# Scores on quarters of the array, a hand-computed order up to chunk 2, and left-over tokens kept on chip

## The chip, the cores and the metric

The kernel runs on one core of one Trainium2 chip. The metric is the device time of one execution in microseconds (us), the median over the runs of one kernel. A profiled execution of the same kernel has a time of its own. Within it the span runs from the first to the last instruction.

## The reference: what is computed

Three layers follow one another, all in float32: windowed attention and two gated feed-forward layers.

```python
# attention: q, k, v are (4, 8, 576, 64) = batch, head, token, head width
scores = q @ k.T / 8
# heads 0-3: keys 0..31 back; heads 4-7: keys 0..127 back, every fourth one
attn = softmax(where(mask, scores, -1e9)); a = attn @ v
x = a.transpose(0, 2, 1, 3).reshape(2304, 512)
# layer 1: w1, w2 (512, 1024), w3 (1024, 1024), w_out (1024, 512)
x = ((x @ w1) * (x @ w2)) @ w3 @ w_out
# layer 2: w_gate, w_val (512, 1536), w_out (1536, 512)
return (silu(x @ w_gate) * (x @ w_val)) @ w_out
```

The weights arrive as float64. Each matrix is kept as a high part and a rest, and a product is three matmuls: high by high, high by rest, rest by high (`mm3`, lines 225 to 227).

## The kernel before, in words

**Stages.** The product W = w3 @ w_out of layer 1 is computed first, in sixteen steps of twelve matmuls over 512 columns (`w_step`). Layer 1 then runs over five chunks of tokens, four of 512 and one of 256 (`stage1`). For each of eight slices k of the inner width a chunk has a gate `w1` (twelve matmuls), a gate `w2` (twelve) and a contraction with W (twelve). So a step of W, a gate or a contraction is twelve matmuls of 512 columns; the text calls it a unit. The W product is 16 units and each of the chunks 0 to 3 is 24. Layer 2 (lines 703 on) works with seven products in place of eight on quarters of the matrices. Its operands are made during layer 1 and kept in DRAM (`quarters`, eighteen blocks of weights, of which chunks 0 to 4 take 3, 4, 4, 5 and 2).

**Attention.** Sixteen pairs of heads, four to a batch. A pair's 576 queries are nine blocks of 64, each against 96 keys. `scores` computes one block of both heads in one matmul: the queries of the two heads stand side by side in a zero-padded 128-row tile, so the 128x128 array holds 64 rows of head 0 and 64 of head 1, with zeros in the other halves. A float32 matmul is two instructions in the trace. The scores are done in two groups, of five blocks and of four; then come mask and scale (DVE, line 344), maximum (347), exponential (ACT, 349), sum and reciprocal (352, 353), normalising (354; DVE for the first batch, POOL later), transposes on PE in three groups (367) with an ACT copy each, the product with v (382, in two groups, each matmul on half of the array's columns), and the split into high part and rest as the layer's input x (167, 168).

**Batches and chunks.** A batch has 576 tokens and a chunk 512, so each batch leaves 64 to 256 tokens for the next chunk. They go to DRAM (`x1d`, line 411) and are read back in front of the next chunk (`load_block`, kind x1).

**Conversion.** A block of weights is 1 MB, two float64 matrices of 128x512. One block takes an ACT pass (208) and two DVE passes (209, 210) to make float32, then an ACT pass (203) and a DVE pass (204) to split it. Twenty blocks are converted before and in chunk 0: eight of w3 and w_out pieces, four of further w3 pieces, eight of (w1, w2).

**Order.** The functions are called in program order; the compiler layer then orders each engine's instructions by its own timeline. All steps of W and the whole first batch of attention are called before the first gate:

```python
for s, step in enumerate(W_STEPS):
    while n_split[0] < min(W_NEEDS[s] + 1, N_W1) and free:
        next_block()
    w_step(*step)
    attend(min(4 * s + 5, done_at[1]))
attend(done_at[1])
```

In chunks 0 to 2 `between` calls pieces of the next batch's attention between the gates and contractions, and `rest` calls weight conversion behind them. SP issues nearly all DMAs from one queue; the stores of layer 1's result are issued by ACT. `stage1(3)` and `stage1(4)` and layer 2 follow.

Of the kernel before, what the change touches and what calls it, by code (L numbers as in the profile page):

```python
# [19 lines left out]
NT = B * S  # L20
# [3 lines left out]
P = 128  # L24
# [6 lines left out]
NBLK = S // QB  # L31
KT = DM // P
# [11 lines left out]
N_EARLY = 15  # L44

ATT_BY = 0.75


W_ORDER = [(("wo1", j), ("w3a", j)) for j in range(2)]
for _name, _j in ("w3c", 0), ("wo1", 2), ("w3a", 2), ("wo1", 4), ("w3a", 4), ("w3c", 2), ("wo1", 6), ("w3a", 6), ("w3d", 0), ("w3d", 2):  # L50
    W_ORDER.append(((_name, _j), (_name, _j + 1)))

W_STEPS = [("w3a", 0), ("w3a", 1), ("w3c", 0), ("w3c", 1), ("w3a", 2), ("w3a", 3), ("w3a", 4), ("w3a", 5),
           ("w3c", 2), ("w3c", 3), ("w3a", 6), ("w3a", 7)] + [("w3d", _j) for _j in range(4)]
W_NEEDS = [1, 2, 3, 4, 5, 5, 7, 7, 8, 9, 10, 10, 11, 11, 12, 12]
W_ORDER += [(("w1", k), ("w2", k)) for k in range(K1)]
# [23 lines left out]
NPROD = 7  # L80
A11, S1, S2, A12, S3, S4, A22 = range(NPROD)
# [8 lines left out]
QUARTERS = [3, 4, 4, 5, 2]  # L90


def moe_chain_kernel(tc, q_in, k_in, v_in, w_in, mask_in, out):
# [8 lines left out]
    with static as st, other as ot, psum as pp, dram as dp:  # L102
# [7 lines left out]
        wslot = [w_all[:, i] for i in (2, 3, 7, 4, 0, 6, 1, 5)] + [fp.tile([P, 2, 2, 512], F32R, name=f"W{i}") for i in range(4)]  # L110
# [3 lines left out]
        ost = [ot.tile([P, S], F32, name=f"o{i}") for i in range(2)]  # L114
        bank = [pp.tile([P, 512], F32, name=f"bk{i}") for i in range(8)]
        acc, ba, bb, batt = bank[:4], bank[4], bank[5], bank[6:]
        x1d = dp.tile([KT, P, NT], F32, name="x1d")
# [8 lines left out]
        for c, n in enumerate(QUARTERS):  # L126

            blocks += [("x1", c + 1)] if c < 4 else []
            blocks += [("w", i + j) for j in range(n)]
            i += n  # L130
# [3 lines left out]
        slot_of, pair_of, uses, raw_at = {}, {}, {}, {}  # L134
        free, raw_free = deque(), deque()

        x1_there = set()

        def load_block():
            n = n_loaded[0]  # L140
            if n == len(blocks) or not raw_free or (blocks[n][0] == "x1" and blocks[n][1] not in x1_there):
                return
# [4 lines left out]
            if kind == "w":  # L147
                dst = r.rearrange("p (b f) -> p b f", b=2)
                src = w_in[i]
            else:  # L150
                if kind == "x1":
                    a, size, ms = CHUNKS[i][0], REST * i, slice(0, KT)
                else:
                    a, size, ms = i[0] * TOK, TOK, slice(2 * i[1], 2 * i[1] + 2)
                dst = r[:, :(ms.stop - ms.start) * size].rearrange("p (m t) -> p m t", t=size)
                src = (x1d if kind == "x1" else x2d)[ms, :, a:a + size].rearrange("m p t -> p m t")
            for b in (0, 1) if n == 0 else (slice(None),):
                nc.sync.dma_start(out=dst[:, b], in_=src[:, b].bitcast(U32))

        def done_with(n):  # L160

            if any(raw_at[n] is r for r in raw[:2]) or n_loaded[0] < (N_W1 if raw_at[n] is raw[2] else N_EARLY):
                raw_free.append(raw_at[n])
# [11 lines left out]
        def next_block():  # L175
            n = n_split[0]
            n_split[0] += 1
            kind, i = blocks[n]
            if kind == "w":
                convert_weights(n, W_ORDER[i])  # L180
            else:
                size = REST * i
                r = raw_at[n].rearrange("p b f w -> p (b f w)")[:, :KT * size].bitcast(F32)
                r = r.rearrange("p (m t) -> p m t", m=KT)
                for m in range(0, KT, 2):
                    x = x_of(i)[:, :, m:m + 2, :size]
                    to_parts(r[:, m:m + 2], x[:, 0], x[:, 1])
            done_with(n)
# [741 lines left out]
```

## Time and profile before

| | us |
|---|---|
| median of 3 runs (lowest, highest) | 848.9 (845.47, 849.26) |
| the profiled execution's own time | 847.58 |
| its span | 845.6 |
| PE busy (x4954) | 825.4 (98% of the span) |
| weight loads busy (x4954) | 751.7 (89%) |
| DVE busy (x957) | 539.6 (64%) |
| ACT busy (x1009) | 429.4 (51%) |
| POOL busy (x124) | 89.2 (11%) |
| DMA | 207.09 MB, mean 245 GB/s |

PE is TensorE, DVE VectorE, ACT ScalarE, POOL GpSimd and SP the engine that issues DMAs. Matmuls are pipelined and their ends are modelled: a matmul of 512 columns is listed with about 0.39 us while the next one starts about 0.23 us later, so what one costs is read from start to start. Idle times of an engine stand with the instruction that ended the wait.

### The profile page before, as it was taken

What the parts mean: (1) busy time and instruction counts of PE and PEld (TensorE: products, weight loads), DVE (VectorE), ACT (ScalarE), POOL (GpSimd) and SP (SyncE); (2) the same over time, 40 slices, a digit from 0 to 9 for tenths busy, and PEclk for the clock granted to TensorE, in tenths of its full rate; (3) what the DMA queues carried; (4) which work ended last, traced back from release to release, by engine and by line L of the source; (5) the groups of instructions that cost most, each with busy time, mean ns of one, the idle gap of its engine ahead of it and who ended that gap; (6) DMA issues with size and microseconds to landing.
All of it is one profiled execution on the core that took longest, in us unless ns stands there. A gap on an engine that the chain in (4) does not pass through costs nothing.

```text
span 845.6 us, 13394 instructions
## 1 busy us (share of the span) xinstructions
PE 825.4 (98%) x4954; PEld 751.7 (89%) x4954; DVE 539.6 (64%) x957; ACT 429.4 (51%) x1009; POOL 89.2 (11%) x124
## 2 busy tenths in 40 slices
PE   7899899999999999999999999999999999999998
PEld 5777788888788788888899999999999999999997
DVE  5899856365626652476766646588655668464867
ACT  5688765455644645254555544354453454353532
POOL 1000134225510642000000000000000000000000
PEclk9999899999999999999999999999999999999999
DMA  9998638558756665567999877788978687887735
GB/s 271 340 354 252 217 88 263 178 171 273 223 164 203 208 209 165 192 223 245 324 299 370 299 253 248 249 289 281 327 249 270 230 266 248 297 283 249 248 102 174
DMA packets 93248, 207.09 MB, mean 245 GB/s; under 512 B 7424, under 2 KB 56704, under 8 KB 88448
## 3 DMA queue, kind: packets, MB, share of 16 engines
q1 hardware_dynamic: 90304, 201.53, 72.5%
q10 hardware_dynamic: 2880, 4.72, 1.6%
q8 instruction: 39, 0.64, 0.3%
q14 instruction: 25, 0.20, 0.1%
HBM read 162.45 MB, written 43.78 MB: 244 GB/s over the span
## 4 chain that ended last, share of the span: by engine, by line
PE 75%; DMA 9%; DVE 9%; ACT 4%; issue 2%; SPq 0%; ACTq 0%; DVEq 0%
PE bk L225 23%; PE bk L226 23%; PE bk L227 23%; DMA raw<-w_in 6%; PE bk L330 2%; ACT s L349 2%; DVE raw L210 2%; PE bk L382 2%; DVE w L204 1%; PE bk L367 1%; DVE raw L209 1%; DVE u L530 1%; DMA q<-q_in 1%; DMA raw<-x1d 1%; DVE early L210 1%
## 5 line engine op out<-in xcount | busy, mean ns | idle before, releaser
L225 PE MATMUL bk<-x,w 128*128 128x512 f32 (+2 forms) x400 | 146.6, 368 | 4.4 <-ACT ta L244 2.2
L226 PE MATMUL bk<-x,w 128*128 128x512 f32 (+2 forms) x400 | 146.7, 367 | 0.0
L227 PE MATMUL bk<-x,w 128*128 128x512 f32 (+2 forms) x400 | 146.4, 366 | 0.0
L225 PE MATMUL bk<-w 128*128 128x384 f32 (+1 forms) x264 | 92.3, 355 | 2.6 <-ACT w L203 2.6
L226 PE MATMUL bk<-w 128*128 128x384 f32 (+1 forms) x264 | 93.5, 354 | 0.8 <-DVE w L204 0.8
L227 PE MATMUL bk<-w 128*128 128x384 f32 (+1 forms) x264 | 90.3, 351 | 0.0
L225 PEld LDWEIGHTS bk<-x,w 128*128 128x128 f32 x400 | 75.5, 189 | 14.6 <-ACT ta L244 2.9
L797 DVE TENSOR_TENSOR acc<-bk,acc 128x384 f32<-128x384 f32 x102 | 55.8, 553 | 44.7 <-PE bk L227 44.5
L226 PEld LDWEIGHTS bk<-x,w 128*128 128x128 f32 x400 | 75.7, 189 | 9.7 <-DVE x L168 0.2
L227 PEld LDWEIGHTS bk<-x,w 128*128 128x128 f32 x400 | 75.7, 189 | 9.6
L227 PE MATMUL bk<-po,wo 128*128 128x384 f32 x240 | 80.6, 336 | 0.0
L226 PE MATMUL bk<-po,wo 128*128 128x384 f32 x240 | 80.3, 335 | 0.0
L225 PE MATMUL bk<-po,wo 128*128 128x384 f32 x240 | 79.5, 336 | 0.3 <-DVE acc L797 0.3
L530 POOL TENSOR_TENSOR stage<-raw,stage 128x256 fp32r<-128x256 f32 x88 | 62.5, 738 | 55.2 <-ACT stage L529 55.0
L722 ACT ACTIVATE u<-bk 128x384 f32<-128x384 f32 x80 | 38.6, 489 | 53.6 <-PE bk L227 53.6
L167 ACT ACTIVATE po<-u 128x768 fp32r<-128x768 f32 (+1 forms) x64 | 50.9, 803 | 26.2 <-PE bk L227 10.5
L208 ACT ACTIVATE raw<-raw 128x1024 f32<-128x1024 f32 (+1 forms) x33 | 37.3, 1130 | 51.6 <-DMA raw<-w_in 51.5
L168 DVE TENSOR_TENSOR po<-u,po 128x768 fp32r<-128x768 f32 (+1 forms) x64 | 57.4, 901 | 8.7 <-ACT po L167 8.6
L226 PE MATMUL bk<-p,W 128*128 128x512 f32 (+1 forms) x160 | 59.2, 374 | 0.0
L227 PE MATMUL bk<-p,W 128*128 128x512 f32 (+1 forms) x160 | 58.7, 371 | 0.0
L225 PE MATMUL bk<-p,W 128*128 128x512 f32 (+1 forms) x160 | 57.8, 375 | 0.1
L349 ACT ACTIVATE s<-s,sm 128x96 f32<-128x96 f32 x144 | 52.0, 364 | 11.4 <-DVE sm L347 11.0
(122 smaller groups left out, 1711.5 us busy)
## 6 DMA issues: line engine op xcount, KB each, us to landing
w<-wd SPq DMA_DIRECT2D x70, 512.0 KB, 4.4
wo<-wod SPq DMA_DIRECT2D x63, 512.0 KB, 4.6
raw<-w_in SPq DMA_DIRECT2D x31, 1024.0 KB, 9.5
mid<-wd SPq DMA_DIRECT2D x42, 512.0 KB, 4.6
wd<-stage SPq DMA_DIRECT2D x16, 896.0 KB, 6.5
wd<-u SPq DMA_DIRECT2D x8, 896.0 KB, 5.6
x<-wd SPq DMA_DIRECT2D x14, 512.0 KB, 4.7
v<-v_in SPq DMA_DIRECT2D x16, 432.0 KB, 8.1
```

What stands on the lines that cost most here:

```text
L167: nc.scalar.activation(hi, src, AF.Copy)
L168: return nc.vector.tensor_tensor(out=lo, in0=src, in1=hi.bitcast(F32), op=ALU.subtract)
L208: nc.scalar.activation(hi.bitcast(F32), hi.bitcast(F32), AF.Prelu, scale=REBIAS, alpha=SIGN_UP)
L210: nc.vector.scalar_tensor_tensor(out=lo, in0=hi, scalar=3, in1=lo, op0=ALU.logical_shift_left, op1=ALU.bitwise_or)
L225: nc.tensor.matmul(ps, wh, xh, start=start, stop=False, skip_group_check=onto)
L226: nc.tensor.matmul(ps, wh, xl, start=False, stop=False, skip_group_check=onto)
L227: nc.tensor.matmul(ps, wl, xh, start=False, stop=stop, skip_group_check=onto)
L330: nc.tensor.matmul(ps[:, (n - b0) * KW:(n - b0 + 1) * KW], q[:, QB + 2 * QB * n:QB + 2 * QB * (n + 1)], kk[:, n * QB:n * QB + KW], start=T ...
L349: nc.scalar.activation(s[:, n], s[:, n], AF.Exp, bias=m[:, 0, n:n + 1], accum_out=m[:, 1, n:n + 1])
L530: (nc.gpsimd if len(stages) == 2 else nc.vector).tensor_tensor(out=dst[:, :, 1], in0=src, in1=dst[:, :, 0].bitcast(F32), op=ALU.subtract)
L722: nc.scalar.activation(t, src, AF.Copy)
L797: nc.vector.tensor_tensor(out=a, in0=ps, in1=a, op=ALU.add)
```

## The change

Four things change, all before chunk 3.

1. **Scores on quarters.** The zero padding of the queries goes, with the memsets on POOL and one of two loads per pair. Each block of each head is a matmul of its own, 64 rows by 64 columns of the array: the head chooses the row half and the PSUM bank, the block's parity the column half. There are 18 such matmuls per pair in place of nine, issued in one go over two banks. The values are likewise issued in one go instead of two. Mask, maximum and so on now run per column group (four and five columns).
2. **An order computed in the kernel.** Everything up to the end of chunk 2 is built as nodes with an engine, an estimated time, what it comes after, and a due time. A list scheduler simulates the five engines and the DMA with those times and starts, on each free engine, the ready node with the earliest due time. The resulting order is issued as it is, without the compiler layer's reordering. Chunks 3 and 4 and layer 2 are still ordered by that layer.
3. **Another sequence.** The blocks of weights are ordered so that (w1, w2) 0 and 1 come third and fourth. Gates of chunk 0 are due from 36 us on and alternate with steps of W: two steps of W, then the gates k = 0 and 1, then again steps of W and gates k = 2, 3, and the rest of W, with results of four gates kept. Attention takes four PSUM banks until the first gate, then two. Quarter blocks in chunks 0 to 4 are 2, 5, 5, 4, 2.
4. **Left-over tokens on chip.** They stay in an SBUF tile `beyond` and are split from there; the DRAM tensor `x1d`, its stores and loads go. Stores of layer 1's result in chunks 0 to 2 are issued by SP in place of ACT.

```diff
-            def scores(i, g):
-                b0, b1 = (0, 5) if g == 0 else (5, 9)
-                for n in range(b0, b1):
-                    nc.tensor.matmul(
-                        ps[:, (n - b0) * KW:(n - b0 + 1) * KW],
-                        q[:, QB + 2 * QB * n:QB + 2 * QB * (n + 1)],
-                        kk[:, n * QB:n * QB + KW],
+            def scores(i, got):
+                q, kk = qd[i % 2], ks[i % 2]
+                for j, n in [(j, 2 * c + (z + j) % 2) for c in range(NHALF) for z in range(2) for j in (1, 0)] + [(1, NBLK - 1), (0, NBLK - 1)]:
+                    h = slice(j * D, (j + 1) * D)
+                    c, z = column(j, n)
+                    c = NHALF if n == NBLK - 1 else c % NHALF
+                    nc.tensor.matmul(
+                        banks_of[got[j]][z * QB:(z + 1) * QB, c * KW:(c + 1) * KW],
+                        q[h, n * QB:(n + 1) * QB], kk[h, n * QB:n * QB + KW],
                         start=True, stop=True,
                     )
...
+W_BLOCKS = [("wo1", 0, 10), ("w3a", 0, 4), ("w1", 0, 0), ("w1", 1, 1), ("wo1", 2, 11), ("w3a", 2, 5), ("w1", 2, 2),
+            ("wo1", 4, 6), ("w3a", 4, 8), ("w1", 3, 3), ("wo1", 6, 7), ("w3a", 6, 9),
+            ("w3b", 0, 4), ("w3b", 2, 5), ("w3b", 4, 4), ("w3b", 6, 5)] + [("w1", _k, _k) for _k in range(4, K1)]
-QUARTERS = [3, 4, 4, 5, 2]
+QUARTERS = [2, 5, 5, 4, 2]
+DMA_RATE = 0.31
+FIRST, EACH, START = 4, 6, 36.0
...
+            def run_nodes(stock):
+                wanted = [x["key"] for x in nodes]
+                for i in reversed(range(len(nodes))):
+                    for a in nodes[i]["after"]:
+                        wanted[a] = min(wanted[a], wanted[i] - nodes[a]["us"] - (4.0 if nodes[a]["mb"] else 0.2))
...
+                    for e in ready:
+                        if free[e] > t + 1e-9:
+                            continue
+                        for i in sorted(ready[e], key=lambda i: (wanted[i], i)):
...
+                            started.append(i)
+                            free[e] = t + x["us"]
...
+                with tc.manual_schedule(engines=set(ENGINES)):
+                    for i in started:
+                        x = nodes[i]
+                        x["f"](*x["args"], **({"got": x["got"]} if x["take"] else {}))
...
+            q_loads(0, 0)
+            mask_at = [node("SP", 0.47, load_mask, slice(0, NHALF), mb=0.2, key=0.1)]
+            for n in range(2):
+                conversion(n, 0.2 + 0.1 * n)
+            q_loads(1, 1)
+            v_loads(0, 2)
+            attention(0, FIRST, 6, mask_at)
...
+            gates(0, 0)
+            gates(0, 1)
+            for j in (2, 4):
+                w_steps(0, (j,), next_at())
+                w_steps(0, (j + 1,), next_at())
+                gates(0, 2 + (j - 2) // 2)
+            w_steps(0, (6, 7), next_at(2))
...
+            for i in range(NPAIR):
+                q_loads(NPAIR + i)
+                v_loads(NPAIR + i)
+                attention(NPAIR + i, START + T * (12 + 5 * i), 3 * T, started_gates)
...
+            def beyond_parts(c, key):
+                size = REST * c
+                ends = []
+                for m in range(0, KT, 2):
+                    before = x_at[c - 1][:] + x_use.get(c - 2, []) + ([raw_use[2], raw_use[3]] if c == 1 else [])
+                    h = node("ACT", on_act(2 * size), x1_part, c, m, 0, after=before, key=key)
+                    ends.append(node("DVE", on_dve(2 * size), x1_part, c, m, 1, after=[h], key=key))
...
-                if g == 1:
-                    nc.sync.dma_start(out=x1d[hp, :, b * S + own:(b + 1) * S], in_=o)
```

## Rows read from the trace of the kernel before

**Rows 1.** Busy time by stretch: stretch, its length, engines, PEclk, DMA share, GB/s.
```profile
0.00:40.00 40.00, 32.76 (x176) 24.22 (x177) 28.41 (x50) 23.25 (x56) 3.22 (x12) 0.91 1.00 300
40.00:100.00 60.00, 54.36 (x356) 44.16 (x355) 58.48 (x90) 50.35 (x101) 0.00 (x0) 0.94 0.82 270
100.00:347.00 247.00, 245.02 (x1594) 202.41 (x1593) 127.17 (x256) 131.99 (x419) 85.97 (x112) 1.00 0.62 198
347.00:450.00 103.00, 101.28 (x581) 89.91 (x580) 70.77 (x147) 50.72 (x111) 0.00 (x0) 1.00 0.80 265
450.00:846.00 396.00, 392.00 (x2254) 391.04 (x2252) 254.79 (x416) 173.12 (x323) 0.00 (x0) 1.00 0.77 259
```

**Rows 2.** Timeline of PE, 0 to 92 us: start, us, instruction [idle before it <- what ended that].
```profile
9.73 3.43 PE L330 MATMUL bk<-k,q 128*128 128x96 f32 x18 [2.32 <-DMA q<-q_in]
...
27.40 0.68 PE L225 MATMUL bk<-w 128*128 128x512 f32 x1 [1.54 <-ACT w L203]
...
89.75 1.22 PE L225 MATMUL bk<-x,w 128*128 128x512 f32 x2 [2.13 <-ACT x L167]
```

**Rows 3.** The same around the end of chunk 2.
```profile
349.50 0.39 PE L227 MATMUL bk<-p,W 128*128 128x512 f32 x1
349.73 0.39 PE L225 MATMUL bk<-x,w 128*128 128x512 f32 x1
...
354.49 0.39 PE L225 MATMUL bk<-x,w 128*128 128x512 f32 x1
```

**Rows 4.** The same around one group each of scores, transposes and values.
```profile
120.61 2.14 PE L330 MATMUL bk<-k,q 128*128 128x96 f32 x18
122.54 0.48 PE L225 MATMUL bk<-x,w 128*128 128x512 f32 x1
...
103.84 0.49 PE L367 MATMUL bk<-ident,s 128*96 128x128 f32 x3
104.08 0.48 PE L225 MATMUL bk<-p,W 128*128 128x512 f32 x1
104.40 0.39 PE L226 MATMUL bk<-p,W 128*128 128x512 f32 x1
...
75.93 0.39 PE L225 MATMUL bk<-w 128*128 128x512 f32 x1
76.25 1.39 PE L382 MATMUL bk<-pt,v 96*64 96x64 f32 x40
77.57 0.50 PE L226 MATMUL bk<-w 128*128 128x512 f32 x1
77.91 0.39 PE L227 MATMUL bk<-w 128*128 128x512 f32 x1
```

**Rows 5.** DVE by line, 0 to 100 us: instruction xcount | busy us, mean ns | idle before.
```profile
L204 DVE TENSOR_TENSOR w<-raw,w 128x1024 fp32r<-128x1024 f32 (+1 forms) x15 | 17.2, 1148 | 1.4 <-ACT w L203 1.3
L210 DVE SCALAR_TENSOR_TENSOR raw<-raw 128x1024 uint32<-128x1024 uint32 (+1 forms) x15 | 17.2, 1148 | 1.1 <-ACT raw L208 0.7
L209 DVE TENSOR_SCALAR raw<-raw 128x1024 uint32<-128x1024 uint32 (+1 forms) x15 | 9.8, 651 | 5.8 <-DMA raw<-w_in 5.8
...
L344 DVE SCALAR_TENSOR_TENSOR s<-bk,mask 128x384 f32<-128x384 f32 (+2 forms) x15 | 6.9, 484 | 3.0 <-PE bk L330 3.0
L347 DVE TENSOR_REDUCE sm<-s 128x5 f32<-128x480 f32 (+1 forms) x10 | 5.9, 595 | 0.0
L168 DVE TENSOR_TENSOR W<-bk,W 128x512 fp32r<-128x512 f32 x8 | 5.4, 680 | 0.0
L354 DVE TENSOR_TENSOR s<-s,sm 128x480 f32<-128x480 f32 (+1 forms) x8 | 4.8, 602 | 0.1
...
L168 DVE TENSOR_TENSOR x<-bk,x 128x256 fp32r<-128x256 f32 (+2 forms) x8 | 4.1, 514 | 0.0
L352 DVE TENSOR_SCALAR sm<-sm 128x5 f32<-128x5 f32 (+1 forms) x9 | 1.5, 162 | 0.1
L353 DVE RECIPROCAL sm<-sm 128x5 f32<-128x5 f32 (+1 forms) x8 | 1.4, 179 | 0.2
```

More of the change, by code (lines that the diff above doesn't have):

```diff
@@ L1 @@
+import heapq
 import math
@@ new lines, in moe_chain_kernel, with node, on_act @@
+            INF = float("inf")
+            def node(engine, us, f, *args, after=(), key=INF, mb=0.0, take=None, give=None, retire=False):
+                nodes.append(dict(
+                    engine=engine, us=us, f=f, args=args, after=[a for a in after if a is not None], key=key, mb=mb,
+                    take=take, give=give, retire=retire, got=None,
+                ))
+                return len(nodes) - 1
+            def on_act(n, in_psum=False):
+                return (0.64 * n + 170 if in_psum else 0.714 * n + 215) / 1000
@@ new lines, in moe_chain_kernel, with next_at, gates @@
+            for n in range(2, 12):
+                conversion(n, after=[q_use[0]])
+            for j in range(2):
+                w_steps(0, (j,), W_AT[j])
+            T = 2.95
+            at = [START]
+            def next_at(n=1):
+                at[0] += n * T
+                return at[0] - n * T
+            def gates(c, k):
+                gate(c, k, next_at(2), T)
+            gates(0, 0)
[4 more added lines that the diff above has]
+                gates(0, 2 + (j - 2) // 2)
@@ new lines, in moe_chain_kernel, with stage1, fin @@
+            beyond_parts(4, at[0])
+            run_nodes({"bank": [0, 1, 2, 3], "o": [0, 1]})
+            n_split[0] = n_loaded[0] = n
+            raw_free.clear()
+            raw_free.extend(raw[(n + j) % 2] for j in range(2))
+            def stage1(c, after):
+                first, n = CHUNKS[c]
+                x = x_of(c)[:, :, :, :n]
+                for k in range(K1):
+                    gate_a(("w1", k), x, n, AF.Copy)
+                    p = gate_b(("w2", k), x, n)
+                    flush()
+                    def fin(k=k, p=p):
+                        contract(slot_of["W", k], p, n, k == 0, k == K1 - 1)
+                        if k == K1 - 1:
+                            drain(lambda m: x2d[m, :, first:first + n], n)
+                    pend.append(fin)
+                    after(k)
@@ new lines, in last_of, with rest @@
+            def last_of(c):
+                first, n = CHUNKS[c]
+                contract_mm(c, K1 - 1, range(KT))
+                drain(lambda m: x2d[m, :, first:first + n], n)
+            pend.append(lambda: last_of(2))
+            count["p"] = 1
+            stage_pool.__exit__(None, None, None)
+            def rest(k):
+                load_block()
+                if k == 0:
+                    load_block()
+                if k == 1:
+                    work.extend([quarters() for _ in range(QUARTERS[3])])
+                if k >= 1:
```

713 lines of the change are left out of this document (459 added, 254 removed).

## The prediction

> **What bounds the kernel now.** I read the busy times by stretch first. From 100 us to the end PE is busy all but 2 to 4 us in each long stretch at full clock (PEclk 1.00), so nothing is to be won there by hiding things better: a gain must take work off PE. In the first 100 us it is different: PE misses 13 us, DVE is busy 58.48 of the 60 us from 40 to 100, and the clock is 0.91 and 0.94 [rows 1]. I then read PE's timeline: the first scores wait for the query load until 9.73 us, and later waits name ACT's weight split and the split of x, behind which stand DVE chains [rows 2]. So the kernel is PE-bound from 100 us on, and bound by DVE and loads before.
>
> The point to compare is the end of chunk 2. Its last contraction ends where the next matmul starts, at 349.73 us; before that, 200 first matmuls of a gate's four have begun, that is 50 gates, and chunks 0 to 2 have 48. A matmul of 512 columns takes (354.49 - 349.73)/21 = 0.2267 us [rows 3], a unit of twelve 2.72 us. Without the two gates of chunk 3 the end of chunk 2 is 349.73 - 5.44 = 344.3 us. That holds 16 units of W, 72 of layer 1 and 16 pairs of attention.
>
> **The change part by part.**
>
> *Scores.* Eighteen instructions on the full array take 122.54 - 120.61 = 1.93 us, 107 ns each [rows 4]. After the change there are 36, each on a quarter. The trace of before shows no quarter. One at a time they would take 36 x 107 = 3.86 us, two at a time 1.93, four at a time 0.96. The nearest row is the values: 40 instructions that alternate between two column halves take 77.57 - 76.25 = 1.32 us, 33 ns each [rows 4], which gives 36 x 33 = 1.19. I take 1.1, between that and 0.96, and keep 0.96 and 3.86 as ends. Around each group the neighbours cost more than 0.227: 104.40 - 104.08 = 0.32 after transposes (0.09 more), 76.25 - 75.93 = 0.32 before and 77.91 - 77.57 = 0.34 behind values (0.09 and 0.11) [rows 4]. The scores came in one or two groups (taken as 1.5), the values too; now one each. A pair before: scores 1.93 + 1.5 x 0.09, transposes 3 x (0.24 + 0.09), values 1.32 + 1.5 x 0.2, together 4.7 us. After: 1.1 + 0.2, 0.99, 1.32 + 0.2, together 3.8. I charge the quarters the values' 0.2 for entering and leaving.
>
> The Trainium skill says in TensorEngine Tiling (Array Packing), Tiling Modes, that tiles load weights and run matmuls independently, but that changing the tiling mode drains the engine. The first half by itself would make the scores 0.96 and the sum 12 x 0.14 = 1.7 us lower; the second speaks against the change, since the scores now enter another mode, and the trace prices such a change for column halves at the 0.2 us charged above. The same page's Gotcha 1 says that row tiles can't use one PSUM bank at once; the heads, which are the row halves, write two banks here, and were they held up all the same, that is the rival below in which the quarters take turns.
>
> *The front.* The first gate needs three blocks of weights and four pairs of attention. On DVE a block is 1.148 + 1.148 + 0.651 = 2.95 us. A pair, from the sums of five pairs (lines 344, 347), four (354, 168 into x, 353) and four and a half (352), is 1.38 + 1.18 + 1.20 + 1.03 + 0.35 + 0.33 = 5.47 us [rows 5]. Together 4 x 5.47 + 3 x 2.95 = 30.7 us. DVE can start about 7 us: the first scores came at 9.73 [rows 2] behind a block of 1 MB, which is some 3.5 us at 300 GB/s [rows 1] and now comes after queries and keys; then about 1 us of scores. So DVE ends at 38 and the first gate starts at about 39 us. Listed durations overlap by some 0.08 us from one instruction to the next, so 35 is the lower end. If DVE is kept only as busy as before, 28.41 of the 35 us after its first block [rows 1], it is 7 + 30.7/0.81 = 45. Loads: four pairs (1 MB each), masks and three blocks are 8 MB, 27 us at 300 GB/s: under it, though not by much. Two steps of W lie in this time.
>
> *From there.* PE still has 86 units, 233.9 us, and 12 pairs at 3.8, 45.7 us. In the next 14 units (38 us of PE, to the end of the first half of W) DVE must do nine blocks (26.6), four splits of W (4 x 0.68 [rows 5] = 2.7) and eight passes of gates of about that length (5.4), together 34.7. It is 91% full, so I charge 4 us of waits, with 1 and 8 as ends. Behind that I charge 2 us, as from 100 to 347 [rows 1]. The clock of 0.94 over 60 us is a loss of 3.6; with fewer waits I take half, 1.8 (0 to 3.6). End of chunk 2: 39 + 233.9 + 45.7 + 4 + 2 + 1.8 = 326.4 us, 17.9 less than 344.3.
>
> *Costed at nothing.* The 'beyond' tile takes stores and loads from SP's queue, and the splits stay; from 100 us on PE waits for nothing of that kind, so it is worth nothing there (and its missing transfers can't cost). Stores of results on SP instead of ACT: four per chunk stand behind a drain, and the loads queued behind them are issued up to some us later; DMA share is 0.62 in that stretch [rows 1], and the cover is the time a raw buffer is filled ahead; without it one load, some 3.5 us, shows per chunk. The normalising on POOL is as before. Chunks 3 and 4 have 4 and 2 quarter blocks in place of 5 and 2: less for DVE, which is not late there (70.77 of 103 us [rows 1]). Layer 2 is the same, PE busy 392 of 396 us [rows 1], so everything behind chunk 2 moves as a whole.
>
> **Sum.** Against the profiled execution's 847.6 us (span 845.6, 2 around it): 847.6 - 17.9 = 829.7 us. The runs shown have a median of 848.9, 1.3 above that execution. The own range: with the low ends 35 + 233.9 + 12 x 3.7 + 1 + 1 + 0 = 315, the high ones with scores at 1.19: 45 + 233.9 + 12 x 3.9 + 8 + 2 + 3.6 = 339; so 818 to 843, and not all ends at once, 820 to 840.
>
> **The rivals.**
>
> *Everything fits.* Four quarters at once, DVE full from the start, hardly a wait: 315, that is 818 us. For it: the rows of values show that two halves do overlap. Against: DVE at 91% with a fixed order. Chance 0.2.
>
> *The front stays DVE's.* The first gate comes at 45 us and DVE, not PE, sets the pace until W is done, another 6 us: 829.7 + 12 = 842. For it: DVE is full from 40 to 100 us now, and the same conversions are only reordered. Against: half of W and most blocks no longer stand in front of the first gate. Chance 0.16.
>
> *The fixed order makes PE wait (slower).* PE takes its instructions in one order, worked out from estimates in which a pair of attention costs 3.1 us of PE (1.05 for scores, 3 x 0.27, 1.25 for values in the nodes' times) and the loads run at 310 GB/s. If each of the 24 steps k of chunks 0 to 2 finds one operand late (a score group queued on PE behind a mask pass on DVE, with the gate behind it), the price is 24 times the wait. From 0.75 us a step the 17.9 us are gone; at 1 us the time is 829.7 + 24 = 854. For it: only two PSUM banks are left for attention after the first gate, and the scores take both. Against: PE is slower than estimated (3.8 to 3.1), so the other engines are early, and the present order waits 2 us in 247. Chance 0.08.
>
> *The quarters take turns (slower).* Scores at 3.86 make a pair 6.6: 39 + 233.9 + 78.8 + 7.8 = 359.5, 863 us. It decides from 2.6 us of scores per pair, 72 ns per instruction, on. For it: no row shows row halves at work together; against: column halves are. Chance 0.06.
>
> **How the numbers follow.** The forecast has 0.50. What a measurement tells from no change is 0.5%, 4.2 us: below 843.4 is faster, above 851.8 slower. Faster: the forecast, the case in which everything fits and 0.10 of the third, 0.80. Slower: the two last, less 0.01, 0.13. The rest, 0.07, is no change. The range goes to the low case and a little past the one with DVE: 817 to 846.
>
> **What would show it.** Scores: 36 instructions of the score line between two neighbours in about 1.1 us; near 1.9 or 3.9 refutes the step. Front: the first gate's matmul at about 39 us, with DVE busy nearly throughout before it. Waits: PE's idle time from 39 to 100 us at about 4 us, and 2 from there to the end of chunk 2, which comes at about 326. Tail: from there on 500 us, as before. The prediction is wrong if the idle time of PE after 100 us is over 10 us, if the first gate comes after 45, or if the tail grows.

## The result and the profile after

The changed kernel takes 840.92 us, the median of five runs (839.0 to 843.04), beside 848.9 us (845.47 to 850.98) for the kernel before: a ratio of 0.9895, interval 0.9866 to 0.9925. It is 8.0 us faster where 17.9 were forecast. Its profiled execution took 842.12 us, 1.2 above that median, with a span of 839.9.

The busy times by stretch answer to [rows 1], with the same columns:

```profile
0.00:40.00 40.00, 24.23 (x281) 17.14 (x281) 27.74 (x66) 25.68 (x86) 0.82 (x8) 0.81 0.97 293
40.00:100.00 60.00, 56.42 (x303) 46.70 (x304) 50.77 (x66) 40.18 (x57) 0.00 (x0) 0.90 0.67 227
100.00:347.00 247.00, 241.65 (x1847) 193.68 (x1846) 149.52 (x301) 145.33 (x449) 96.22 (x120) 0.99 0.65 217
347.00:450.00 103.00, 102.28 (x599) 91.97 (x598) 64.63 (x133) 46.63 (x102) 0.00 (x0) 1.00 0.72 242
450.00:840.00 390.00, 386.09 (x2218) 385.45 (x2216) 252.85 (x412) 170.97 (x318) 0.00 (x0) 1.00 0.77 257
```

The first row carries the miss. PE is busy only 24.23 of 40 us, and its granted clock is 0.81 where it was 0.91. DVE is busy 27.74; it starts at 7.21 us, as forecast, and from there to the first gate it is busy 36.77 of 43.41 us. The third row has a smaller miss: PE misses 5.35 us where it missed 2.

PE's timeline answers to [rows 2]. First the front (start, us, instruction, idle before it and what ended that):

```profile
15.80 1.86 PE L290 MATMUL bk<-k,q 64*64 64x96 f32 x36 [8.64 <-DMA q<-q_in]
...
26.86 1.04 PE L290 MATMUL bk<-k,q 64*64 64x96 f32 x36
...
36.84 2.30 PE L337 MATMUL bk<-ident,s 128*96 128x128 f32 x9 [4.14 <-ACT early L181]
40.76 2.40 PE L355 MATMUL bk<-pt,v 96*64 96x64 f32 x40 [1.62 <-ACT pt L341]
43.10 1.09 PE L337 MATMUL bk<-ident,s 128*96 128x128 f32 x4
45.53 1.27 PE L337 MATMUL bk<-ident,s 128*96 128x128 f32 x5 [1.34 <-ACT x L579]
48.28 2.40 PE L355 MATMUL bk<-pt,v 96*64 96x64 f32 x40 [1.48 <-ACT pt L341]
50.62 0.80 PE L193 MATMUL bk<-x,w 128*128 128x512 f32 x1
```

Line 290 is the scores, 337 the transposes, 355 the values; the last row is the first gate, at 50.62 us where 39 was forecast. PE waits 8.64 us for the second pair's queries; after the third pair's scores (26.86) it has little but attention to do and waits at four places for more than 1 us for what ACT and DVE make of it. In these waits the clock falls (granted 0.50 from 40 us to the gate): the same 40 values that take 1.32 us elsewhere [rows 4] take 43.10 - 40.76 = 2.34. DVE is busy 22.18 of the 23.76 us from the third scores to the gate. By the gate it has made float32 of six blocks of weights and split five, where the forecast counted three; and the DMA has moved 293 GB/s x 40 us = 11.7 MB by 40 us, where it counted 8.

Now a score group, and the end of chunk 2 (for [rows 3] and [rows 4]):

```profile
278.12 0.39 PE L195 MATMUL bk<-x,w 128*128 128x512 f32 x1
278.44 1.04 PE L290 MATMUL bk<-k,q 64*64 64x96 f32 x36
279.41 0.50 PE L193 MATMUL bk<-x,w 128*128 128x512 f32 x1
279.75 0.39 PE L194 MATMUL bk<-x,w 128*128 128x512 f32 x1
...
343.45 0.39 PE L195 MATMUL bk<-p,W 128*128 128x512 f32 x1
```

Thirty-six quarter instructions take 279.41 - 278.44 = 0.97 us, 27 ns each; the neighbours take 278.44 - 278.12 = 0.32 and 0.34, that is 0.09 and 0.11 over 0.227, as charged. The last contraction of chunk 2 ends at 343.45 + 0.23 = 343.68, with a gate and a half of chunk 3 in front of it (4.08): the end of chunk 2, counted as before, is 339.6 us. The forecast was 326.4, before it was 344.3.

Last, the place behind the 5.35 us of the third stretch. These rows are PE's, DVE's and SP's queue, in this order:

```profile
264.91 0.88 PE L337 MATMUL bk<-ident,s 128*96 128x128 f32 x3 [2.97 <-POOL s L329]
265.44 0.78 PE L193 MATMUL bk<-x,w 128*128 128x512 f32 x1
266.02 0.63 PE L194 MATMUL bk<-x,w 128*128 128x512 f32 x1
...
270.71 0.89 PE L337 MATMUL bk<-ident,s 128*96 128x128 f32 x6
...
249.68 1.72 DVE L582 TENSOR_TENSOR x<-beyond,x 128x384 fp32r<-128x384 f32 x2
255.52 0.70 DVE L183 TENSOR_SCALAR raw<-raw 128x1024 uint32<-128x1024 uint32 x1 [4.12 <-DMA raw<-w_in]
256.13 1.44 DVE L301 SCALAR_TENSOR_TENSOR s<-bk,mask 128x384 f32<-128x384 f32 x4
...
241.41 4.73 SPq L838 DMA_DIRECT2D wd<-stage  x2
246.23 0.51 SPq L570 DMA_DIRECT2D raw<-w_in  x1
```

Read them upwards. The load of a quarter block is issued at 246.23 us behind two stores, and lands at 255.5, 9.3 us later. DVE's next instruction in the fixed order is that block's first pass, and it stands idle for 4.12 us with the mask pass of the scores queued behind it. The normalising, and with it the transposes, come that much later, and PE waits 2.97 us. The page names POOL as the releaser, but POOL is only the last link. Behind the wait twelve matmuls take 270.71 - 265.44 = 5.27 us, where they take 2.72 at full clock: another 2.5.

### The profile page after: what moved, and what is told of

Same layout as the page of the kernel before. It is cut to its first block, busy times and chain, and to the rows that moved or that the text cites. A ratio compares the mean times of both kernels' runs of the same rounds, so it can differ in the third digit from the quotient of the medians.

```text
span 839.9 us, 13927 instructions
## 1 busy us (share of the span) xinstructions
PE 810.7 (97%) x5242; PEld 734.9 (88%) x5242; DVE 545.5 (65%) x976; ACT 428.8 (51%) x1011; POOL 97.0 (12%) x128
## 4 chain that ended last, share of the span: by engine, by line
PE 75%; DMA 9%; DVE 8%; ACT 6%; issue 1%; SPq 1%; POOL 0%; ACTq 0%; DVEq 0%; POOLq 0%
PE bk L193 24%; PE bk L195 23%; PE bk L194 23%; DMA raw<-w_in 7%; ACT s L318 2%; PE bk L355 2%; PE bk L337 1%; DVE raw L820 1%; DVE raw L185 1%; DMA q<-q_in 1%; DVE s L301 1%; ACT raw L181 1%; PE bk L290 1%; ACT stage L831 1%; DVE sm L313 1%
## 5 line engine op out<-in xcount | busy, mean ns | idle before, releaser
L195 PEld LDWEIGHTS bk<-x,w 128*128 128x128 f32 x400 | 76.0, 190 | 10.7
L833 POOL TENSOR_TENSOR stage<-raw,stage 128x256 fp32r<-128x256 f32 x96 | 71.4, 777 | 32.3 <-ACT stage L831 32.2
L193 PE MATMUL bk<-w 128*128 128x384 f32 (+1 forms) x216 | 73.1, 341 | 0.0
L194 PE MATMUL bk<-w 128*128 128x384 f32 (+1 forms) x216 | 73.1, 338 | 0.0
L195 PE MATMUL bk<-w 128*128 128x384 f32 (+1 forms) x216 | 72.5, 339 | 0.0
L181 ACT ACTIVATE raw<-raw 128x1024 f32<-128x1024 f32 (+1 forms) x32 | 34.9, 1090 | 30.0 <-DMA raw<-w_in 30.0
```

The lines of the kernel that those rows point to most:

```text
L181: nc.scalar.activation(hi.bitcast(F32), hi.bitcast(F32), AF.Prelu, scale=REBIAS, alpha=SIGN_UP)
L193: nc.tensor.matmul(ps, wh, xh, start=start, stop=False, skip_group_check=onto)
L194: nc.tensor.matmul(ps, wh, xl, start=False, stop=False, skip_group_check=onto)
L195: nc.tensor.matmul(ps, wl, xh, start=False, stop=stop, skip_group_check=onto)
L833: nc.gpsimd.tensor_tensor(out=dst[:, :, 1], in0=src, in1=dst[:, :, 0].bitcast(F32), op=ALU.subtract)
```

## The experiments

Each is an edit of the changed kernel unless it says otherwise. Each was timed beside the kernel before, whose medians were 848.8 to 850.7 us.

### What the gain is made of

**Scores on the whole array, in the same order.**

```diff
-                for j, n in [(j, 2 * c + (z + j) % 2) ...] + [(1, NBLK - 1), (0, NBLK - 1)]:
+                for j, c in [(j, c) for c in range(NHALF + 1) for j in (1, 0)]:
+                    n = min(2 * c, NBLK - 2)
...
-                        q[h, n * QB:(n + 1) * QB], kk[h, n * QB:n * QB + KW],
+                        q[:, n * QB:(n + 2) * QB], kk[:, n * QB:n * QB + KW],
```

> The changed kernel in the same order, but the scores of a pair are ten matmuls on the whole array (twenty instructions) in place of eighteen on quarters; what they compute is not the scores, only their number and places count. Theory (the measured gain of 8 us is the shorter scores and nothing else): a score group takes 20 x 107 ns = 2.1 us in place of 0.97, without the 0.1 us for entering and leaving another mode, so 12 pairs behind the first gate cost 12 x (2.14 - 0.97 - 0.2 + 0.09) = 12.7 us: about 854 us, ratio 1.005, no gain left or a little slower. Rival (PE has slack in this order, as its waits show, and the order and the sequence are worth something by themselves): at most half of it shows, under 847 us, ratio 0.997 or less.

Measured: 852.0 us (ten runs), ratio 1.0034 [1.0017, 1.0051]. The theory holds in the main (854 was expected): the quarters are worth 852.0 - 840.9 = 11.1 us, more than the whole gain. A group on PE's timeline:

```profile
202.76 2.37 PE L288 MATMUL bk<-k,q 128*128 128x96 f32 x20
204.90 0.48 PE L193 MATMUL bk<-x,w 128*128 128x512 f32 x1
```

That is 2.14 us for twenty instructions, 107 ns each as before. With the eighteen that the kernel before had, sixteen pairs would be 16 x 0.21 = 3.4 us shorter, an estimate of 848.6 us: the time of the kernel before. So sequence, order and left-over tokens together are worth about nothing, and the whole gain is the scores. This holds in the new order; scores on quarters in the old order were not run.

**Quarters in turn.** The same instructions, sorted so that a head's even blocks come first, then its odd ones, then the other head's.

```diff
-                for j, n in [(j, 2 * c + (z + j) % 2) ...] + [(1, NBLK - 1), (0, NBLK - 1)]:
+                for j, n in [(j, n) for j in (1, 0) for z in range(2) for n in range(z, NBLK, 2)]:
```

> The kernel after, with the 18 score matmuls of a pair sorted so that all of one quarter of the array stand behind one another. If the gain of the scores is that four quarters work at once, a group of 36 instructions takes 1.9 us (54 ns each, weights of 64 columns) to 3.9 us (107 ns each) instead of 0.97, and the kernel is 12 x 0.95 = 11 to 35 us slower. If the smaller tile alone makes it cheap, the group stays near 1 us and the time the same.

Measured: 856.7 us, 1.0083 [1.0052, 1.0113].

```profile
205.31 2.36 PE L290 MATMUL bk<-k,q 64*64 64x96 f32 x36
207.60 0.50 PE L193 MATMUL bk<-x,w 128*128 128x512 f32 x1
...
277.95 0.53 PE L337 MATMUL bk<-ident,s 128*96 128x128 f32 x3 [0.44 <-POOL s L329]
```

A group takes 2.29 us, 64 ns each. Twelve pairs behind the first gate make 12 x (2.29 - 0.97) = 15.8 us, and 856.7 - 840.9 = 15.8 is what it costs. That the two agree to the tenth is chance. In the profiled execution the first gate comes 3.6 us later than in the changed kernel (54.23), and from there to the end of chunk 2 it takes 10.2 us longer, not 15.8: the stall of the changed kernel at 264 us, 2.97 us and 2.5 of lowered clock, has shrunk to the 0.44 us above. 15.8 less these 5 us is 10.7. With the scores on the whole array it is the same: gate at 53.81, 7.8 us more behind it where 12.7 were expected, and 0.63 us left of the stall. It is the order of issue over the quarters that makes the gain: in turn the change would have been slower than before.

**The same sequence, ordered by the compiler layer.**

```diff
-                with tc.manual_schedule(engines=set(ENGINES)):
-                    for i in started:
+                for i in started:
```

> The kernel after, with the computed order given to the compiler layer as program order, which then orders each engine's instructions by its own timeline as in the kernel before. If the fixed order brings most of what the sequence gains, it is 5 us or more slower than the kernel after. If only the sequence and the quarters matter, it is within 3 us of it. If the fixed order costs waits in the front, it is faster and the first gate earlier than 50 us.

Measured: 899.21 us, 1.0565 [1.0532, 1.0597]; first gate 61.55. Its busy times from 100 to 347 us:

```profile
100.00:347.00 247.00, 220.52 (x1474) 175.22 (x1473) 131.04 (x253) 128.97 (x376) 88.85 (x114) 0.93 0.60 204
```

PE misses 26.5 us of the 247, at a clock of 0.93. The computed order is worth 58 us for this sequence of calls; but the kernel before, with its own sequence in the compiler layer's order, took 849, so that isn't a gain of the change.

### What sets the front

**Fewer bytes in front.** Loads of the first two blocks bring 64 of 512 columns (zeros beside them).

```diff
-                nc.sync.dma_start(out=dst[:, b], in_=src[:, b])
+                cols = slice(0, 128) if n < 2 else slice(None)
+                nc.sync.dma_start(out=dst[:, b, cols], in_=src[:, b, cols])
```

> The kernel after, same order, but the loads of the first two blocks of weights bring 64 of 512 columns (the rest is set to zero), so 0.25 MB stand in the queue in front of the second pair's queries instead of 2 MB. The weights are wrong for that. Theory A (loads set the front): the second scores start near 9 us instead of 15.8 and the first gate at 43 to 45 instead of 50.6. Theory B (DVE and ACT throughput set it): the first gate moves by less than 2 us. Theory C (chains from pair to pair through PE at half clock and two score tiles set it): part of the 7 us arrives, 2 to 5.

Measured: 838.6 us, 0.9865 [0.9824, 0.9906]; the first gate at 47.99, chunk 2 ends at 333.0. The second scores come at 10.46 in place of 15.80, but of these 5.3 us only 2.6 are left at the gate, as theory C had it.

**Less DVE work in front.** The float32 passes of the first four blocks work on 8 columns.

```diff
-            x = to_float32(r, (piece,))
+            if n < 4:
+                to_float32(r[..., :8, :], (piece,))
+                x = r[..., 1].bitcast(F32)
```

> The kernel after, same order, but the three passes that make float32 of the first four blocks of weights touch 8 of 512 columns (the weights are wrong for that). This frees DVE of some 6.5 us and ACT of 4 before the first gate. Theory B (throughput of DVE): the first gate at 44 us instead of 50.6. Theories A and C: it moves by less than 2.5 us.

Measured: 840.66 us, 0.9894 [0.9864, 0.9924]; first gate 52.02. The rows are 0 to 50 us of the changed kernel and of this one:

```profile
0.00:50.00 50.00, 30.65 (x362) 22.57 (x364) 37.26 (x82) 33.40 (x106) 0.82 (x8) 0.75 0.97 294
...
0.00:50.00 50.00, 28.56 (x336) 20.28 (x338) 30.35 (x81) 29.61 (x106) 0.81 (x8) 0.77 0.97 287
```

DVE is busy 7 us less and the gate is no earlier: DVE's work, taken as a sum, isn't what sets the gate.

**PE kept awake.** Thirty-four idle matmuls behind the first scores.

```diff
+            node("PE", 7.4, fill_pe, after=[q_use[0]], key=5)
```

> The kernel after with 34 further matmuls of bfloat16 zeros on PE behind the first scores, where PE waits for the second pair's queries. Theory C (half clock of PE in the front stretches the chains): second scores, transposes and the first steps of W run at full clock and the first gate comes 2 to 4 us earlier. Otherwise, or if the extra matmuls only push the second scores back, it comes at 50 us or later.

Measured: 838.28 us, 0.9872 [0.9835, 0.9909]; first gate 48.34, PEclk 0.85 in place of 0.75 over 0 to 50 us:

```profile
0.00:50.00 50.00, 37.70 (x407) 25.55 (x409) 38.35 (x85) 34.83 (x109) 0.81 (x8) 0.85 0.96 292
...
24.19 1.04 PE L290 MATMUL bk<-k,q 64*64 64x96 f32 x36
```

The second scores start at 15.84, as in the changed kernel (15.80), and the third at 24.19 in place of 26.86. So the clock is 2.3 us of the front, as far as these matmuls reach: they end at 14.6 us, and the values before the gate take 2.3 us as in the changed kernel.

**Later blocks held back**, until the loads of the fourth pair's values are issued; and then with the idle matmuls as well.

```diff
-                conversion(n, after=[q_use[0]])
+                conversion(n, after=[q_use[0] if n < 4 else loads["v", 3]])
```

> The kernel after, but the loads of blocks of weights 4 to 11, which no gate before the third needs, wait until the last v load of the first batch is issued. Theory A2 (the queue of loads sets the front: loads not needed for the first gate stand in front of v of pairs 2 and 3, which land 15.1 and 12.2 us after issue): v lands within 8 us, the values of pairs 2 and 3 start some 5 us earlier, the first gate at 44 to 46 us instead of 50.6. Theory C (chains and conversions interleaved on ACT and DVE): the first gate at 48 us or later. Against a gain in the end: blocks 4 and 5 come later, so PE could wait for them behind the first gates.

> x5 and x3 together: loads of blocks 4 to 11 held back, and 34 matmuls of zeros on PE behind the first scores. If the queue of loads and PE's half clock are two separate causes, their shares add: first gate 5 to 8 us earlier than 50.6, the kernel at 833 to 836 us, which would be the fastest here. If both only feed one chain, it is as x5 or x3 alone.

Measured: 840.26 us, 0.9878 [0.9847, 0.9909], first gate 48.15; with both 837.73, 0.985 [0.9822, 0.9879], first gate 47.53. The values landed 9.2 us after their issue (median), not within 8, and the gate is where theory C had it. The shares of 2.3 to 2.6 us don't add up.

Each gate is read from one execution, and executions differ. Three runs below leave the front as it is: with the normalising on DVE the gate is at 50.77, with short loads of the quarter blocks at 50.74, and with the stores on POOL the second scores and the gate are these:

```profile
13.68 1.86 PE L290 MATMUL bk<-k,q 64*64 64x96 f32 x36 [6.21 <-DMA q<-q_in]
...
48.17 0.80 PE L193 MATMUL bk<-x,w 128*128 128x512 f32 x1
```

There the queries landed 2 us earlier without any edit. So 2.5 us at the gate, alone, is within what one execution can differ from another. By the medians fewer bytes are worth 2.3 us, the idle matmuls 2.6 and the held-back loads 0.7, and the intervals of the three ratios overlap with the changed kernel's. For the clock the rows between second and third scores speak as well. For the held-back loads the stretch from the third scores to the gate does: 21.9 us, where the changed kernel and the three runs above have 23.7 to 23.8. With the idle matmuls added it is 23.9 again, with a wait of 1.8 for a query load in it.

**Loads, DVE passes and clock at once.** Six blocks with short loads, four with short passes, and the idle matmuls; then the same without the matmuls.

```diff
+            if n < 4:
+                to_float32(r[..., :8, :], (piece,))
+                x = r[..., 1].bitcast(F32)
...
+                cols = slice(0, 128) if n < 6 else slice(None)
+                nc.sync.dma_start(out=dst[:, b, cols], in_=src[:, b, cols])
...
+            node("PE", 7.4, fill_pe, after=[q_use[0]], key=5)
```

> Loads of the first six blocks bring 64 of 512 columns (the rest is zero), the float32 passes of the first four work on 8 columns, and 34 idle matmuls stand behind the first scores to keep PE's clock up; the products of the weights are wrong and work is left out. Each of these alone moved the first gate by 2 to 3 us or not at all. Theory (the three together set the front: when one goes, the next is late): the first gate comes at 40 to 42 us, chunk 2 ends 8 us earlier than in the changed kernel, 832 to 834 us. Rival (the fixed order itself: the chain from scores to values of four pairs, two at a time, with steps of the conversions between): the first gate stays at 46 us or later and the time at 837 to 839 us.

> The changed kernel's order, with loads of the first six blocks cut to 64 of 512 columns (zeros beside them) and the float32 passes of the first four on 8 columns; no idle matmuls. The products of the weights are wrong and work is left out. Theory (bytes and DVE work cover for each other: one alone gave 2.6 us, the other nothing): together they bring the first gate to 42 us or earlier and the time to 833 us. Rival (the chain of the four pairs in its fixed order: scores, mask, exponentials, normalising, transposes, values, some 10 us by themselves, the next pair's transposes queued behind scores and steps of W): the first gate stays at 44 us or later, and the time at 835 us or more.

Measured: 835.51 us, 0.9827 [0.9799, 0.9854], first gate 46.20; without the matmuls 838.07, 0.9866 [0.9828, 0.9905], first gate 46.82. The rivals hold for the gate (46 or later, 44 or later); the first kernel's time lay between its two expectations. There the matmuls themselves ran until 15.90 us, with the second scores behind them, so the second kernel is the cleaner one. On its timeline, PE and then DVE:

```profile
23.63 1.04 PE L294 MATMUL bk<-k,q 64*64 64x96 f32 x36
...
28.43 1.04 PE L294 MATMUL bk<-k,q 64*64 64x96 f32 x36
33.07 2.30 PE L341 MATMUL bk<-ident,s 128*96 128x128 f32 x9 [3.60 <-DVE s L333]
36.99 2.40 PE L359 MATMUL bk<-pt,v 96*64 96x64 f32 x40 [1.61 <-ACT pt L345]
39.32 1.09 PE L341 MATMUL bk<-ident,s 128*96 128x128 f32 x4
...
44.49 2.40 PE L359 MATMUL bk<-pt,v 96*64 96x64 f32 x40 [1.48 <-ACT pt L345]
46.82 0.80 PE L197 MATMUL bk<-x,w 128*128 128x512 f32 x1
...
24.86 1.44 DVE L305 SCALAR_TENSOR_TENSOR s<-bk,mask 128x384 f32<-128x384 f32 x4
26.42 1.10 DVE L317 TENSOR_REDUCE sm<-s 128x5 f32<-128x480 f32 x2
29.03 0.17 DVE L327 TENSOR_SCALAR sm<-sm 128x5 f32<-128x5 f32 x1 [1.34 <-ACT s L322]
...
32.37 0.56 DVE L333 TENSOR_TENSOR s<-s,sm 128x384 f32<-128x384 f32 x1
```

Loads are quick here (values land 3.9 us after their issue, in the changed kernel 11.8) and DVE waits for ACT. From the third pair's scores to its transposes it is 33.07 - 23.63 = 9.4 us all the same: mask, maxima, exponentials, sums, normalising, one after the other. The last step stood 1.45 us behind the fourth pair's mask pass (30.88). The fourth pair's transposes start 39.32 - 28.43 = 10.9 us behind its scores. From 23.63 to the gate 23.2 us pass, for two pairs. In the changed kernel it is 50.62 - 26.86 = 23.8. DVE is busy 22.18 us of that stretch there and 19.32 here, so 3 us less of its work makes it 0.6 us shorter. I read it as a chain of steps in the fixed order, not as a sum of work; only what lies before it gets shorter with fewer bytes. Only the held-back loads changed what the order puts into it (43 instructions of DVE in place of 46, 55 of ACT in place of 57, 1.8 us less). No run cleared it of the conversions or kept PE at full clock there (granted 0.68 in the changed kernel, 0.69 here). The two groups of values alone take 2.3 us each in place of 1.3, so some 2 us of it are the clock's, by an estimate from these rows; how much of the rest is the order stays open.

### What stalls at 264 us

**Normalising on DVE** in place of POOL for all batches.

```diff
-                (nc.vector if i < NPAIR else nc.gpsimd).tensor_tensor(
+                nc.vector.tensor_tensor(
```

> The kernel after with the normalising of all batches on DVE instead of POOL. If the wait of 2.97 us at 264.9 us and the half clock behind it (another 1.7) come from the normalising queued on POOL behind stage passes that wait for ACT, the end of chunk 2 comes 3 to 5 us earlier. If DVE is short of time after 100 us (it is busy 60%), new waits take its place and the time is the same.

Measured: 840.94 us, 0.9889 [0.9868, 0.9909]. The wait is there still, and POOL, which the profile named, isn't its cause:

```profile
264.37 0.85 PE L337 MATMUL bk<-ident,s 128*96 128x128 f32 x3 [2.64 <-DVE s L329]
```

**Stores of quarter blocks issued by POOL.**

```diff
-                    stage_use[st] = node("SP", 0.47, stage_store, n, i, st, after=ends, mb=0.92, ...)
+                    stage_use[st] = node("POOL", 0.6, stage_store, n, i, st, after=ends, mb=0.92, ...)
...
-                nc.sync.dma_start(out=dst.bitcast(F32), in_=stages[st]...)
+                nc.gpsimd.dma_start(out=dst.bitcast(F32), in_=stages[st]...)
```

> The stores of the quarter blocks are issued by POOL, behind the sums that it makes for them, in place of SP. Theory (the stall at 264 us starts where SP waits for POOL with a store and issues the next block's load 5 us late): DVE's wait of 4 us for that load goes, the wait of 3 us on PE behind it too, with the lowered clock that follows it: chunk 2 ends 3 to 5 us earlier, 836 to 838 us. Rival (the load is late because of the DMA queues or a free buffer, not of SP's order): the wait stays at 2.5 us or more and the time at 840 to 842 us.

Measured: 857.15 us, 1.0088 [1.0062, 1.0113]: slower by 16 us, which neither theory had. POOL's groups from 100 to 347 us show a cost that I had left out:

```profile
L838 POOL DMA_DIRECT2D wd<-stage x16 | 16.2, 1010 | 3.6 <-POOL stage L833 3.3 <-DMA wd<-stage 0.3
L838 POOL DMA_DIRECT2D wod<-stage x8 | 7.5, 942 | 2.1 <-POOL stage L833 2.1
```

Each store keeps POOL busy for about 1 us, 23.7 us in all, in front of sums and normalising. PE misses 17.0 us from 100 to 347, in many waits. The plan came out in another order as well, so how much of the 16 us is POOL's time and how much the new order stays open. As a test of the stall this run says nothing.

**Short loads of the quarter blocks** in chunks 0 to 2.

```diff
-                nc.sync.dma_start(out=dst[:, b], in_=src[:, b])
+                cols = slice(0, 128) if n >= N_W1 else slice(None)
+                nc.sync.dma_start(out=dst[:, b, cols], in_=src[:, b, cols])
```

> The changed kernel, but the loads of the quarter blocks in chunks 0 to 2 bring 64 of 512 columns (the rest of the buffer keeps old values); layer 2's weights are wrong and bytes are left out. Theory (the stall at 264 us comes from a block's load that lands 9 us after its issue behind 1.8 MB of stores, with the mask pass of the scores queued behind the block's first pass on DVE): DVE's wait of 4.1 us at 251 us goes, PE's of 3.0 us and the lowered clock behind it too: chunk 2 ends 3 to 5 us earlier, 836 to 838 us. Rival (the attention chain is late by itself at this place): the wait stays at 2 us or more and the time at 840 to 842 us.

Measured: 837.7 us, 0.986 [0.9819, 0.9902]. The same place, DVE and PE:

```profile
251.33 1.12 DVE L183 TENSOR_SCALAR raw<-raw 128x1024 uint32<-128x1024 uint32 x1 [0.75 <-DMA raw<-w_in]
253.17 1.45 DVE L301 SCALAR_TENSOR_TENSOR s<-bk,mask 128x384 f32<-128x384 f32 x4 [0.72 <-PE bk L290]
...
261.96 0.53 PE L337 MATMUL bk<-ident,s 128*96 128x128 f32 x3 [0.43 <-POOL s L329]
262.24 0.48 PE L193 MATMUL bk<-x,w 128*128 128x512 f32 x1
```

The mask pass comes 3.0 us earlier, PE waits 0.43 in place of 2.97, and the matmul behind the transposes takes 0.32 to the next one, not 0.58. Chunk 2 ends at 333.8, 5.8 us earlier in the profiled execution; 3.2 in the medians. The stall is the late load, with the mask pass queued behind it.

### What was costed at nothing

**Left-over tokens stored as well.**

```diff
+                nc.sync.dma_start(out=x1d[hp, :, b * S + own:(b + 1) * S], in_=beyond[:, hp, :S - own])
```

> The changed kernel, with the left-over tokens stored to DRAM as well, as before the change (sixteen stores on SP's queue, not read back). Theory (the removed stores were hidden): 840 to 842 us, no difference to the changed kernel. Rival (stores on SP hold up loads queued behind them): from 0.5 us a store on, 8 us more, 849 us.

Measured: 841.52 us, 0.9901 [0.9864, 0.9938]. As forecast, these stores cost nothing. The reads of the tokens weren't put back.

### Versions that put together what helped

**Held back, kept awake, stores on POOL**; then, in place of the stores, **POOL's measured durations in the plan**, without and with the idle matmuls.

```diff
-                        ends.append(node("POOL", {256: 0.7, 128: 0.42}[cols], stage_part, ...))
+                        ends.append(node("POOL", {256: 0.78, 128: 0.5}[cols], stage_part, ...))
```

> A version that puts together what helped: loads of blocks 4 to 11 held until the values' loads of the first four pairs are issued, 34 idle matmuls behind the first scores, and the stores of the quarter blocks issued by POOL. Theory (front and stall are separate losses): the 3 us of the first two (837.7 us) and the 3 to 5 us of the third add up, 833 to 835 us, ratio 0.98. Rival (time won in front is waited for later, since the fixed order was worked out for another pace): 837 us or more, ratio 0.985 or above.

> Loads of blocks 4 to 11 held until the values' loads of the first four pairs are issued, and the planner's times for POOL's sums set to what the trace of the changed kernel shows (0.78 and 0.5 us in place of 0.7 and 0.42). Theory (the plan was too fast for POOL and so put SP's stores and DVE's passes too early): the wait at 264 us goes and the time is 836 to 838 us. Rival (a small change of the plan moves the waits elsewhere): 840 us or more.

> A version from what helped: loads of blocks 4 to 11 held back, 34 idle matmuls behind the first scores, and POOL's measured durations in the plan. Theory (front and stall are separate losses, 2.5 and 2 us): 835 to 837 us, ratio 0.983. Rival (what the front wins is lost at other waits of the fixed order): 838 us or more, as each of them alone.

Measured: the first 855.5 us, 1.0095 [1.0063, 1.0127], for the stores on POOL as above. The second 838.36, 0.9873 [0.9836, 0.9911], between its two expectations: at the old place PE waits 0.48 us, but new waits of 1.8 and 1.7 us stand at 243 and 290 us. The third 835.23 us (834.45 to 838.44), 0.9846 [0.982, 0.9872]. Its first gate:

```profile
46.54 0.80 PE L193 MATMUL bk<-x,w 128*128 128x512 f32 x1
```

Chunk 2 ends at 332.8, PE's longest wait from 100 us on is 1.8 us. It is the quickest of the versions that leave no work out, 1.5% faster than the kernel before by the ratio. Over the changed kernel (840.92) it is 5.7 us by the medians of two sets of runs; the intervals of the two ratios just overlap. That the two losses are separate is what this run speaks for, not more.

## Why the prediction was wrong

It failed at one step, the front. In the profiled execution 842.1 - 829.7 = 12.4 us are missing. The first gate accounts for 50.62 - 39 = 11.6, the stretch from there to the end of chunk 2 for 1.6 (289.0 where 287.4 was forecast), and the rest of the kernel gives back 1 us (839.9 - 339.6 = 500.3, was 501.3).

- **The front, wrong.** "Together 4 x 5.47 + 3 x 2.95 = 30.7 us" and "So DVE ends at 38 and the first gate starts at about 39 us" took the front as DVE's work for what the gate needs, with no gap. The start was right, 7.21 us. But the order puts passes of six blocks before the gate, not three, so DVE had 36.8 us of work, and it stood idle for 6.6. Nor is the work the cause by itself: with 7 us less of it the gate came no earlier (52.02). What the runs show in place of that sum is bytes (2.6 us at the gate when taken away, 2.3 in the median), the lowered clock (2.3 and 2.6), which don't add up, and a stretch from the third pair's scores to the gate that takes 23.8 us, and still 23.2 when loads and passes are cut. That this stretch is the chain of two pairs in the fixed order is read from its timeline; the nearest test of it, the held-back loads, made it 1.8 us shorter, and the rest stays open. The forecast's upper end, 45, had DVE busy for 0.81 of the time. It was busy for 0.85 of it, but with more work than was counted. [Rows 2] had a hint: before the change the first scores already waited for a load, and PE for ACT's splits.
- **Loads, named but mispriced.** "27 us at 300 GB/s: under it, though not by much" compared the 8 MB that the gate needs with the time. By 40 us 11.7 MB had moved, and with the queue full (DMA share 0.97) values landed 11.8 us after their issue (median of five). Without the bytes in front they landed after 3.9 us, and that brought the gate forward by 3.8 us, together with the shorter passes.
- **Scores, right.** 0.97 us where 1.1 was taken and 0.96 the lower end, the entering and leaving as charged. The Trainium skill, TensorEngine Tiling (Array Packing), Tiling Modes, says that tiles work independently; the 27 ns against 64 in turn agree. It also says that a change of mode drains the engine. The 0.20 us around a group are not all such a drain: around a group on the whole array stand 0.09 (0.32 for the matmul at 204.90, 0.23 for the one before the group). The rival in which the quarters take turns had 107 ns an instruction; in turn they took 64.
- **From the first gate on, right in size by luck.** 6 us of waits were charged and 5.1 measured, but of the 4 up to the end of W none came (PE is busy 49.38 of 49.38 us from the gate to 100 us), and of the 2 behind it 5.1 did, most of it the stall at 264 us. The clock cost some 3.5 (0.9 behind the first gate, 2.5 behind the stall), where 1.8 was charged; the scores gave 12 x 0.13 = 1.6 back. Some 2 us of the 289.0 stay unaccounted for.
- **The rival of the fixed order** had its mechanism (a mask pass queued on DVE behind an instruction that waits, PE behind both), but at one step of the 24. The rival of DVE's front came nearest to the time (842), by another road: its gate was at 45 us, and of the 6 us that it had behind the gate none came.
- **The tail, right, and the tokens' stores too.** Both moved nothing. The tokens' reads were not tested.

So the forecast counted two gains, the scores (12 x 0.9 = 10.8 us) and the earlier first gate. Only the first is there. The sequence brings the first gate forward, but W then runs beside chunk 0, and with the old scores the kernel would take its old time.

## What to carry to other kernels

A front is not the sum of what the first result needs on the fullest engine: count also the work for later steps that the order puts before it, write down the chain of one item, step by step, and ask when each load lands behind the queue. In a fixed order look for instructions that wait for a DMA in front of those on the chain of the bound engine. And price a change by undoing one part of it in the new order: here that showed that one of four parts made the whole gain. Add up such a test from its own trace: a match in the total can be two errors that cancel. And before a share is read from one trace, look how far untouched runs differ at the same place.

## What the runs showed of the hardware

- Matmul instructions of 64x64 by 96 columns take 27 ns each when consecutive matmuls (of two instructions) lie on different quarters and 64 ns when one quarter has a run of them; on the whole array the same 96 columns take 107.
- A store issued by POOL kept POOL busy for 0.94 to 1.01 us. The Trainium skill, Perfetto Trace Analysis, DMA Instruction — SWDGE (GPSIMD), says that such an instruction lasts until the descriptors are made, not until the bytes have moved; the trace agrees: these stores landed 8.1 us (`wd`) and 7.3 us (`wod`) after their issue (medians), long after POOL was done with them.
- After the wait of 2.97 us PE's next twelve matmuls ran at half the rate for 5.3 us: the price of that wait was nearly double its length. It is no fixed factor: after the 2.64 us with the normalising on DVE only six matmuls did, in 2.7 us.
